# Attention out of PSUM by pairs of banks, part of the second product in whole float32, and a new order

## The chip, the cores and the metric

The kernel runs on one core of a Trainium2 chip. TensorE multiplies matrices and writes only to PSUM, which has eight banks of 512 float32 columns on 128 partitions. VectorE and ScalarE read PSUM and SBUF, GpSimd (POOL) works on SBUF here, and SyncE issues the transfers (DMA). The engines run side by side, each executes its own list in order, and they wait for each other by semaphores. The metric is the device time of one execution in microseconds (us).

## The reference

```python
def _attn_ref(q, k, v, f_logit):          # 4 batches, 8 heads, 768 steps, 48 wide
    f = 1.0 / (1.0 + np.exp(-f_logit))
    for t in range(S):
        state = f[:, :, t, :, None] * state + np.einsum('bhd,bhe->bhde', k[:, :, t], v[:, :, t])
        y[:, :, t] = np.einsum('bhd,bhde->bhe', q[:, :, t], state)
    return y

def _moe_ref(x, w_in, w_out):             # x: 3072 x 384; w_in: 384 x 2048; w_out: 2048 x 384
    h = x @ w_in
    relu6 = np.clip(h + 3.0, 0.0, 6.0)
    return ((h * relu6 / 6.0) @ w_out).astype(np.float32)
```

The heads of the attention's output, side by side, are `x`. `q`, `k`, `v` and `f_logit` come as float32, both weights as float64.

## The kernel before, in words

**Attention.** The 768 steps are cut into six chunks of 128, and a chunk of one batch is a *unit*: 24 units, numbered chunk by chunk with the four batches inside. A unit is prepared by loads (`load` of the gates, `loadq` of q and k, `loadv`), a sigmoid on ScalarE (`gate`), two scans over the gates on VectorE (`back`, `fwd`), their ends (`rend`), products of keys and queries with the scans (`kmul`, `qmul`), and the decay of the old state (`decay`). On TensorE it then has five steps in plain float32, each of small matmuls on a quarter of the array: `tk` (keys transposed), `kv` (the state's additions), `qs` (queries with the state), `att` (keys with queries) and `av` (the masked result with the values, added onto what `qs` left in PSUM). `ktok` copies the transposed keys out on ScalarE. `mask0` and `mask1` multiply each half of `att`'s result with the causal mask on VectorE. `carry0` and `carry1` add the halves of `kv` to the state, two instructions each, on VectorE (on ScalarE for the first four units).

**Out of PSUM.** The expert layer wants its numbers as a pair of the shorter float32 form (`F32R`): a high part, copied on ScalarE, and a low part, subtracted on VectorE. A unit's output `y` lies in two banks and leaves in three pieces: `xh0`, `xh1`, `y3h` copy (256, 128 and 128 columns) and `xl0`, `xl1`, `y3l` subtract. The last piece goes to a tile of its own, `y3`, from which two DMAs (`hole`) fill the 16 unused rows on two places of the other blocks, so that 4 x 96 rows fill three blocks of 128.

**Expert layer.** The four units of a chunk make a *group* of 512 columns, and there are 6 groups x 16 slices of the hidden width = 96 slices, numbered through. Each has a first product `mm1` (nine matmuls: high x high, high x low and low x high over three blocks), `relu` on ScalarE, `g` on VectorE, the high and low parts of the result (`gh` on ScalarE, `gl` on VectorE), and a second product `mm2` (nine matmuls into three banks that add up over a group). At the end `outs`, `outv` and `od` copy and store; the last group's third output block is split into halves (`mm2a`, `mm2b`).

**Weights.** While the first group runs, 16 slices of float64 weights are turned into pairs: `ld` loads 768 KB into a ring of three buffers, `z` and `cy` (ScalarE) and `mid`, `lim`, `dif`, `top` (VectorE) build the float32 number by integer arithmetic in place, `high` copies the high part on ScalarE and `low` subtracts the low part on VectorE or POOL. A load waits until the `low` that last used its buffer is done.

**Order.** Nothing is scheduled while the kernel is built: the string `ORDER` lists every step, and each engine executes its own in that order. `ON_POOL` names the vector steps that go to GpSimd. The digits behind a TensorE step name the PSUM banks that it writes (five banks, `g0` to `g4`; three more hold the second products' sums). `warm.n` puts n bfloat16 matmuls on zeros into TensorE's list. A step whose bank, tile or input is still in use waits for it.

Of the kernel before, what the change touches and what calls it, by code (L numbers as in the profile page):

```python
# [39 lines left out]
kmul.1 qmul.1 kmul.3 qmul.3 kmul.4 qmul.4 kmul.5 gl.0 decay.5 low.3 kmul.6 decay.6 low.9 kmul.7 decay.7 qmul.7  # L40
kmul.8 gl.13 qmul.8 kmul.9 decay.9 gl.17 kmul.10 kmul.11 qmul.11 qmul.10 kmul.12 decay.12 kmul.13 qmul.13
kmul.14 qmul.14 kmul.15 qmul.15 decay.16 qmul.17 gl.46 gl.51 kmul.19 qmul.19 decay.20 kmul.21 qmul.21 kmul.23
qmul.22 decay.23 qmul.23
""".split()
ORDER = """
load.0 loadq.0 load.1 loadv.0 loadq.1 loadv.2 loadv.1 gate.0 loadq.2 back.0 rend.0 kmul.0 gate.1 fwd.0 warm.13
tk.0.0 ktok.0 kv.0.12 qmul.0 load.2 back.1 carry0.0 carry1.0 qs.0.34 att.0.01 rend.1 kmul.1 mask0.0 loadq.3
mask1.0 av.0 fwd.1 tk.1.2 xh1.0 loadv.3 xh0.0 y3h.0 ktok.1 y3l.0 load.3 qmul.1 xl1.0 xl0.0 kv.1.01 hole.0 gate.2
carry0.1 back.2 carry1.1 warm.2 qs.1.24 ld.0 att.1.30 kmul.2 loadq.4 rend.2 tk.2.1 fwd.2 ktok.2 gate.3 qmul.2
load.4 mask0.1 mask1.1 warm.6 kv.2.13 back.3 av.1 carry0.2 ld.1 xh1.1 y3h.1 rend.3 cy.0 y3l.1 kmul.3 xl1.1  # L50
warm.2 qs.2.04 z.0 fwd.3 xh0.1 carry1.2 mid.0 warm.3 att.2.13 load.5 qmul.3 xl0.1 gate.4 mask0.2 hole.1 tk.3.2
mask1.2 ktok.3 lim.0 av.2 dif.0 loadq.6 kv.3.13 xh0.2 top.0 ld.2 xh1.2 y3h.2 carry0.3 loadv.4 carry1.3 xl0.2
loadv.5 cy.1 xl1.2 qs.3.21 y3l.2 att.3.30 back.4 hole.2 high.0 z.1 low.0 loadq.5 gate.5 mid.1 kmul.4 mask0.3
mask1.3 warm.9 av.3 ld.3 lim.1 tk.4.4 dif.1 y3h.3 loadv.6 xh0.3 ktok.4 top.1 xh1.3 xl1.3 high.1 y3l.3 xl0.3
warm.4 kv.4.30 rend.4 cy.2 hole.3 low.1 z.2 fwd.4 mid.2 load.6 decay.4 qmul.4 carry0.4 ld.4 carry1.4 lim.2
warm.15 qs.4.41 dif.2 att.4.20 top.2 loadq.7 mask0.4 high.2 mask1.4 back.5 cy.3 warm.4 av.4 mm1.0.3 loadv.7
xh1.4 xh0.4 low.2 z.3 xl0.4 kmul.5 y3h.4 ld.5 gate.6 xl1.4 y3l.4 hole.4 mm1.2.2 relu.0 mid.3 lim.3 g.0 dif.3
gh.0 top.3 mm1.1.0 relu.2 g.2 gl.0 cy.4 gh.2 rend.5 mm2.0 relu.1 gl.2 z.4 g.1 decay.5 gh.1 mid.4 lim.4 tk.5.4
high.3 gl.1 ktok.5 dif.4 mm2.1 low.3 mm2.2 top.4 ld.6 fwd.5 cy.5 mm1.3.1 high.4 qmul.5 load.7 z.5 low.4 mid.5
ld.7 mm1.4.3 lim.5 relu.3 dif.5 g.3 top.5 gh.3 kv.5.20 relu.4 gl.3 high.5 g.4 mm2.3 cy.6 low.5 gh.4 carry0.5  # L60
ld.8 z.6 gl.4 mm1.5.4 gate.7 mid.6 lim.6 dif.6 top.6 mm2.4 relu.5 back.6 high.6 cy.7 low.6 qs.5.13 z.7 g.5
kmul.6 ld.9 carry1.5 gh.5 mm1.6.4 mid.7 gl.5 lim.7 dif.7 mm2.5 top.7 relu.6 g.6 high.7 rend.6 gh.6 low.7
att.5.02 cy.8 tk.6.4 gl.6 ld.10 z.8 mask0.5 decay.6 mm2.6 mask1.5 ktok.6 mid.8 lim.8 dif.8 top.8 av.5 fwd.6
mm1.7.0 loadv.8 high.8 cy.9 low.8 load.8 z.9 qmul.6 mm1.8.2 ld.11 relu.7 mid.9 lim.9 xh1.5 y3h.5 g.7 xh0.5 dif.9
gh.7 kv.6.40 top.9 relu.8 gate.8 gl.7 high.9 g.8 mm2.7 cy.10 low.9 carry0.6 y3l.5 xl0.5 gh.8 xl1.5 carry1.6 z.10
hole.5 qs.6.21 gl.8 ld.12 mm1.9.3 mid.10 lim.10 dif.10 top.10 mm2.8 relu.9 back.7 high.10 g.9 cy.11 kmul.7
att.6.04 gh.9 low.10 tk.7.3 z.11 loadq.8 loadq.9 gl.9 ktok.7 ld.14 mid.11 mm1.10.3 lim.11 dif.11 top.11 mask0.6
mm2.9 relu.10 mask1.6 high.11 g.10 gh.10 low.11 cy.12 kv.7.04 gl.10 ld.13 mm1.11.3 z.12 rend.7 fwd.7 mid.12
load.9 decay.7 mm2.10 relu.11 lim.12 qmul.7 carry0.7 g.11 gh.11 dif.12 av.6 top.12 xh1.6 loadv.9 xh0.6 gl.11
high.12 back.8 mm2.11 cy.13 low.12 z.13 gate.9 kmul.8 xl1.6 ld.15 xl0.6 mm1.12.3 y3h.6 carry1.7 y3l.6 mid.13  # L70
hole.6 lim.13 dif.13 top.13 qs.7.20 relu.12 att.7.41 g.12 high.13 loadq.10 mask0.7 tk.8.3 cy.14 low.13 gh.12
mask1.7 mm1.13.4 z.14 gl.12 ktok.8 mid.14 lim.14 dif.14 av.7 relu.13 top.14 kv.8.13 y3h.7 loadv.10 xh1.7 xh0.7
mm2.12 g.13 high.14 xl0.7 gh.13 low.14 cy.15 y3l.7 gl.13 mm1.14.4 xl1.7 z.15 hole.7 mid.15 lim.15 dif.15 mm2.13
relu.14 top.15 g.14 high.15 rend.8 mm1.16.2 gh.14 low.15 gl.14 decay.8 fwd.8 mm1.15.0 relu.16 g.16 qmul.8
load.10 carry0.8 gh.16 carry1.8 mm2.14 relu.15 gl.16 g.15 back.9 gh.15 mm1.17.4 gate.10 gl.15 rend.9 kmul.9
mm2.15 relu.17 decay.9 g.17 fwd.9 gh.17 mm1.18.2 outs.0 outv.1 gl.17 outs.2 load.11 od.0 od.1 qmul.9 mm2.16 od.2
relu.18 back.10 g.18 kmul.10 gate.11 mm2.17 gh.18 back.11 gl.18 mm1.19.1 rend.11 decay.11 mm2.18 relu.19 g.19
gh.19 mm1.20.3 gl.19 mm2.19 relu.20 g.20 gh.20 mm1.21.0 gl.20 mm2.20 relu.21 g.21 gh.21 qs.8.42 gl.21 att.8.13
tk.9.0 mask0.8 loadq.11 mask1.8 ktok.9 mm1.22.1 av.8 relu.22 kv.9.30 xh1.8 loadv.11 g.22 xh0.8 mm2.21 y3h.8
# [20 lines left out]
g.43 qmul.17 load.19 tk.15.4 mm1.44.2 ktok.15 gh.43 rend.18 decay.18 gl.43 av.14 kv.15.34 relu.44 gate.19 g.44  # L100
mm2.43 loadv.17 y3h.14 xh0.14 carry0.15 gh.44 xl0.14 xh1.14 gl.44 xl1.14 y3l.14 mm1.45.2 back.19 hole.14
carry1.15 mm2.44 relu.45 g.45 gh.45 tk.16.1 gl.45 qs.15.03 att.15.42 ktok.16 mask0.15 mm1.46.1 mask1.15 av.15
kv.16.42 relu.46 g.46 xh1.15 mm2.45 xh0.15 xl1.15 gh.46 carry0.16 xl0.15 y3h.15 gl.46 y3l.15 carry1.16 hole.15
# [58 lines left out]
def gla_moe(ctx: ExitStack, tc: tile.TileContext, fg, qk, v, w, outT):  # L162
# [5 lines left out]
    )  # L168
    cv = Ring(ctx.enter_context(tc.tile_pool(name="cv", bufs=1)), {"raw": 3, "y": 1})
# [4 lines left out]
    def bank(shape, name):  # L174
# [621 lines left out]
```

## Time and profile before

| | us |
|---|---|
| median of 3 runs | 520.85 |
| lowest and highest run | 518.43, 521.64 |
| span of the profiled execution | 519.0 |
| TensorE (PE) busy in that span | 499.7 |
| VectorE (DVE) busy | 316.3 |
| ScalarE (ACT) busy | 215.5 |
| GpSimd (POOL) busy | 55.5 |

For the profiled execution the page gives its span, from the first to the last instruction, and no time beside it; the span lies between the lowest and the highest run. A line of the page names the line of the kernel, the engine, the operation, output and input, the shapes and the count; then come the busy time, the mean of one instruction in ns, and the idle time just before with what ended it. PE is matmuls and PEld weight loads, which overlap them. The span of a matmul in the records is longer than its share of TensorE's time, because matmuls are pipelined; the distance from start to start is that share.

### The profile page before, as it was taken

The page shows a single profiled execution, that of the slowest core. Times are in us where ns is not written, and L with a number is a line of the kernel's source. Part 1 is how long each engine was busy: PE and PEld are TensorE (multiplying, and loading weights), DVE is VectorE, ACT ScalarE, POOL GpSimd, SP SyncE. Part 2 cuts the span into 40 slices and gives each one's busy share as a digit, 9 for nine tenths or more (in the row PEclk, how much of TensorE's full clock was granted, in tenths as well). Part 3 has the DMA queues.
Part 4 walks back from the last instruction along what each step waited for, and adds up shares of the span by engine and source line. Part 5 has one row for each costly group of instructions (what it writes and reads, how often), then busy time and mean ns, then how long its engine had stood idle before and what let it go on. Part 6 is the DMA issues. An engine that isn't in the chain of part 4 may idle for free.

```text
span 519.0 us, 11607 instructions
## 1 busy us (share of the span) xinstructions
PE 499.7 (96%) x4931; PEld 391.9 (76%) x4931; DVE 316.3 (61%) x599; ACT 215.5 (42%) x390; POOL 55.5 (11%) x61
## 2 busy tenths in 40 slices
PE   7889999989999999999999999999999999999995
PEld 3556777668877777888788778778777778888884
DVE  6799999998936768334783476547364333333331
ACT  3466676666433434333333343334233233433341
POOL 3213111212202112000200002000040000000000
PEclk9799999989999999999999999999999999999998
DMA  8886445741204223300320422111230000200002
GB/s 240 242 259 204 140 134 165 255 125 42 80 1 123 53 65 92 97 0 25 98 70 16 115 77 58 39 52 35 64 105 11 12 1 8 62 1 2 0 1 66
DMA packets 24554, 41.97 MB, mean 81 GB/s; under 512 B 2480, under 2 KB 17072, under 8 KB 24496
## 3 DMA queue, kind: packets, MB, share of 16 engines
q1 hardware_dynamic: 24496, 41.15, 26.9%
q8 instruction: 41, 0.67, 0.6%
q14 instruction: 17, 0.14, 0.1%
HBM read 34.07 MB, written 4.72 MB: 75 GB/s over the span
## 4 chain that ended last, share of the span: by engine, by line
PE 82%; DVE 8%; ACT 4%; issue 3%; DMA 1%; SPq 0%; POOL 0%; DVEq 0%; ACTq 0%; POOLq 0%
PE h L528 36%; PE o L565 33%; PE y L465 3%; PE o_half L577 2%; PE y L451 2%; PE at L378 2%; PE tk L400 2%; PE kv L419 2%; DVE raw L263 1%; DMA raw<-w 1%; PE idle L660 1%; ACT top L243 1%; ACT weight L268 1%; DVE gg L551 1%; DVE top L259 1%
## 5 line engine op out<-in xcount | busy, mean ns | idle before, releaser
L528 PE MATMUL h<-xt,weight 128*128 128x512 f32 x864 | 220.5, 401 | 2.2 <-ACT raw L234 1.2
L565 PE MATMUL o<-gg,weight 128*128 128x512 f32 x816 | 208.7, 399 | 0.3 <-ACT gg L547 0.3
L528 PEld LDWEIGHTS h<-xt,weight 128*128 128x128 f32 x864 | 160.8, 190 | 40.7 <-ACT top L243 1.3
L565 PEld LDWEIGHTS o<-gg,weight 128*128 128x128 f32 x816 | 151.4, 188 | 36.8 <-DVE gg L551 0.4
L542 DVE SCALAR_TENSOR_TENSOR tg<-tg,h 128x512 f32<-128x512 f32 x96 | 65.9, 686 | 123.7 <-ACT tg L538 123.3
L538 ACT ACTIVATE tg<-h,half 128x512 f32<-128x512 f32 x96 | 66.1, 688 | 178.7 <-PE h L528 176.9
L551 DVE TENSOR_TENSOR gg<-tg,gg 128x512 fp32r<-128x512 f32 x94 | 65.9, 701 | 40.9 <-ACT gg L547 36.9
L547 ACT ACTIVATE gg<-tg 128x512 fp32r<-128x512 f32 x96 | 60.6, 632 | 58.2 <-DVE tg L542 57.4
L326 POOL TENSOR_TENSOR qkf<-qkf,suffix 112x512 f32<-112x512 f32 x17 | 23.2, 1363 | 249.1 <-DVE tg L542 96.1
L313 DVE TENSOR_TENSOR_SCAN suffix<-gates,unit 112x516 f32<-112x516 f32 x24 | 30.3, 1261 | 3.0 <-ACT gates L307 2.8
L333 DVE TENSOR_TENSOR_SCAN suffix<-gates,rend 112x516 f32<-112x516 f32 x24 | 30.1, 1253 | 0.8 <-POOL qkf L326 0.5
L339 POOL TENSOR_TENSOR qkf<-qkf,suffix 112x512 f32<-112x512 f32 x15 | 18.0, 1202 | 42.9 <-DVE suffix L333 39.2
L388 DVE TENSOR_TENSOR a<-at,causal 128x256 f32<-128x256 f32 x48 | 18.1, 416 | 7.3 <-PE at L378 7.1
L465 PEld LDWEIGHTS y<-a,v 64*48 64x48 f32 (+1 forms) x768 | 13.4, 124 | 10.8 <-issue 6.2
L407 ACT ACTIVATE ktok<-tk 128x448 f32<-128x448 f32 (+1 forms) x24 | 12.3, 512 | 19.5 <-PE tk L400 19.4
L465 PE MATMUL y<-a,v 64*48 64x64 f32 (+1 forms) x768 | 17.5, 225 | 2.1 <-DVE a L388 2.0
L263 DVE SCALAR_TENSOR_TENSOR raw<-top,raw 128x768 int16<-128x768 int16 x16 | 18.2, 1138 | 0.5
L378 PE MATMUL at<-qkf 48*64 48x64 f32 x768 | 17.1, 227 | 1.4 <-ACT state L438 1.4
L660 PE MATMUL idle<-blank 128*128 128x512 bf16 x58 | 17.2, 445 | 1.1 <-DVE blank L198 1.1
L268 ACT ACTIVATE weight<-raw 128x768 fp32r<-128x768 f32 x16 | 13.5, 845 | 10.8 <-DVE raw L263 10.8
L496 ACT ACTIVATE xt<-y 112x128 fp32r<-112x128 f32 (+1 forms) x48 | 14.0, 327 | 9.1 <-PE y L465 9.1
L419 PE MATMUL kv<-v,ktok 64*48 64x48 f32 (+1 forms) x768 | 16.2, 216 | 1.6 <-ACT ktok L407 1.4
(61 smaller groups left out, 307.9 us busy)
## 6 DMA issues: line engine op xcount, KB each, us to landing
raw<-w SPq DMA_DIRECT2D x16, 768.0 KB, 5.2
qkf<-qk SPq DMA_DIRECT2D x24, 448.0 KB, 4.4
gates<-fg SPq DMA_DIRECT2D x24, 226.2 KB, 2.9
v<-v SPq DMA_DIRECT2D x24, 200.0 KB, 3.5
outT<-os SPq DMA_DIRECT2D x17, 256.0 KB, 3.1
xt<-y SPq DMA_DIRECT2D x48, 48.0 KB, 2.2
outT<-os SPq DMA_DIRECT2D x2, 128.0 KB, 3.4
```

The lines of the kernel that those rows point to most:

```text
L263: nc.vector.scalar_tensor_tensor(upper, conv[f]["y"], 8.0, upper, op0=ALU.mult, op1=ALU.add)
L313: nc.vector.tensor_tensor_scan(flat(sf)[:, ::-1], gt[:, 1:][:, ::-1], flat(unit)[:, ::-1], 0.0, op0=ALU.mult, op1=ALU.add,)
L333: nc.vector.tensor_tensor_scan(flat(sf), gt[:, :NP * (C + 1)], flat(rend), 0.0, op0=ALU.mult, op1=ALU.add,)
L378: nc.tensor.matmul(d["ps"][e][HC * odd:HC * (odd + 1), 2 * n + c], t[rs, 1, n, c, odd], t[rs, 0, n, c, odd], start=True, stop=True,)
L419: nc.tensor.matmul(d["kv"][odd][r:r + m, c, n], d["ktok"][rs, 2 * n + part, r:r + m], heads_of(vt[rs], part, n, e)[:, :D], start=(odd, e) ...
L465: nc.tensor.matmul(d["y"][odd][to:to + m, n, cs], heads_of(vt[rs], c, n, e)[:, :m], d["a"][rs, 2 * n + c, e], start=False, stop=True, skip ...
L528: nc.tensor.matmul(h, win[:, f, a, k * 128:(k + 1) * 128], g["xt"][:, k, :g["n"] // C, b], start=i == 0, stop=i == 3 * KT - 1,)
L538: nc.scalar.activation(d["t"], d["h"], AF.Relu, bias=half, scale=1.0 / 6.0)
L542: nc.vector.scalar_tensor_tensor(d["t"], d["t"], 1.0, d["h"], op0=ALU.min, op1=ALU.mult)
L547: nc.scalar.activation(d["gg"][:, 0], d["t"], AF.Copy)
L551: engine("gl", f if g["name"] == "0" else NU).tensor_tensor(d["gg"][:, 1], d["t"], d["gg"][:, 0].bitcast(F32), op=ALU.subtract)
L565: nc.tensor.matmul(g["o"][m], wout[:, f, a, m * 128:(m + 1) * 128], g[f]["gg"][:, b], start=f == 0 and i == 0, stop=f == NF - 1 and i == 2 ...
```

## The change

The five working banks become one tile `work`, and steps take one bank or two neighbouring ones of it. The two banks of `att`, of `kv` and of `y` are such pairs, so that one instruction reads both: `mask` takes the place of `mask0` and `mask1`, `xh` of three copies, `xl` of three subtractions, and `carry0` and `carry1` have one instruction instead of two. `y` uses columns 0 to 255 of its pair and `kv` columns 256 to 447 of its pair, and the order puts both into banks 0 and 1 for most units. The piece that fills the unused rows goes to a fourth block of the group's input. All blocks lie in one tile of seven, of which even groups use the first four and odd ones the last four from the end, so the middle one belongs to both. `decayed` has two buffers instead of one for each batch. `av` begins with an instruction that does nothing and waits until `qs` is done.

In the first eight slices of the first group, `mm2x` takes the place of `gh`, `gl` and `mm2`: three matmuls in whole float32, of the gated result itself and whole weights. For them the DMA `wd` puts the second half of a slice's float32 weights where its low part will be, `lowi` makes the low part of the first half, and `lowo` later makes that of the second half in place. The raw ring has two buffers instead of three, and the float32 weights get two of their own.

The order and `ON_POOL` are new. Fillers (`warm`) go from 58 to 46. Steps that issued transfers stay one for one, but for eight `wd` that are added, and stand at other places. Of the vector steps `kmul` 13 (before 17), `qmul` 13 (15), `decay` 13 (8), two `gl` (2), two `low` (2), two `lowi` and one `lowo` are on POOL.

```diff
-        {"qkf": 3, "v": 3, "ktok": 2, "y3": 2, "tg": 4, "gg": 3, "a": 1, "xt": 2},
+        {"qkf": 3, "v": 3, "ktok": 2, "tg": 4, "gg": 3, "a": 1},
-    cv = Ring(..., {"raw": 3, "y": 1})
+    cv = Ring(..., {"raw": 2, "w": 2, "y": 1})
+    work = ps_g.tile([128, 5, 512], F32, name="work")
+    def bank():
+        return work[:, banks.pop(0) if banks else 0]
+    def pair():
+        n = banks.pop(0) if banks else 0
+        return work[:, n:n + 2]
...
+    def conv_low(op, f, cols, whole):
+        engine(op, f).tensor_tensor(
+            weight[:, f, 1, cols], whole, weight[:, f, 0, cols].bitcast(F32), op=ALU.subtract
+        )
+    def conv_keep(f):
+        nc.sync.dma_start(out=weight[:, f, 1, OUTS].bitcast(F32), in_=conv[f]["w"][:, OUTS])
+        "low": lambda f: conv_low("low", f, slice(0, WN), conv[f]["w"]),
+        "lowi": lambda f: conv_low("lowi", f, INS, conv[f]["w"][:, INS]),
+        "lowo": lambda f: conv_low("lowo", f, OUTS, weight[:, f, 1, OUTS].bitcast(F32)),
...
-        def mask(e):
+        def mask():
+            nc.vector.tensor_tensor(
+                d["a"].rearrange("r p e t -> r e p t"), d["at"],
+                causal.unsqueeze(1).unsqueeze(1).broadcast_to([128, 2, NP, HC]), op=ALU.mult,
+            )
...
+            d["kv"] = pair()[:, :, 256:256 + 4 * D].rearrange("r o (c n d) -> r o c n d", c=2, n=2)
+            d["y"] = pair()[:, :, :2 * C].rearrange("r o (n t) -> r o n t", t=C)
...
         def av():
             vt = values[i]
+            hold = nc.tensor.nop()
+            after(hold.ins, d["qs"], mybir.DependencyClass.Sync)
...
+        def parts(low):
+            return rows_of(g)[:PR, :, j, low].rearrange("r (n o) t -> r o n t", o=2)
+        def xh():
+            nc.scalar.activation(parts(0), d["y"][:PR], AF.Copy)
+        def xl():
+            nc.vector.tensor_tensor(parts(1), d["y"][:PR], parts(0).bitcast(F32), op=ALU.subtract)
...
+            g["xt"] = xts[:, KT:][:, ::-1] if g["odd"] else xts[:, :KT + 1]
...
+    def mm2_whole(g, f):
+        for m in range(KT):
+            nc.tensor.matmul(
+                g["o"][m], wout[:, f, 1, m * 128:(m + 1) * 128].bitcast(F32), g[f]["t"],
+                start=f == 0, stop=f == NF - 1, skip_group_check=True,
+            )
```

Of the order, the start, the stretch around units 8 to 10, and that around unit 18; in the old order the first product stood behind `warm.4 av.4`:

```diff
+load.0 loadq.0 loadv.0 loadq.1 load.1 loadv.1 loadv.2 gate.0 loadq.2 back.0 ld.0 ld.1 rend.0 kmul.0 warm.15 tk.0.4
...
+xh.3 xl.3 high.1 back.4 hole.3 gate.5 wd.1 cy.2 ld.3 lowi.1 loadv.6 mid.2 lim.2 warm.10 mm1.0.4 dif.2 top.2 ld.4
+back.5 high.2 wd.2 mm1.1.0 relu.0 lowi.2 g.0 kmul.5 cy.3 rend.4 mm1.2.4 relu.1 kmul.4 z.3 g.1 decay.4 mid.3 mm2x.0
...
+att.9.2 decay.10 loadq.11 av.8 gl.21 kv.9.0 loadv.11 mask.9 mm2.20 xh.8 carry0.9 xl.8 carry1.9 hole.8 qs.9.0 kmul.11
+att.10.2 loadq.12 decay.11 av.9 fwd.11 kv.10.0 tk.11.4 xh.9 mm2.21 rend.12 load.13 ktok.11 xl.9 qmul.11 hole.9
...
+att.18.2 loadq.20 av.17 kv.18.0 decay.19 mask.18 loadv.20 mm2.57 xh.17 carry0.18 xl.17 carry1.18 hole.17 tk.19.4 gh.58
+kmul.20 qs.18.0 ktok.19 gl.58 att.19.2 loadq.21 fwd.20 av.18 kv.19.0 mm2.58 xh.18 carry0.19 qmul.20 load.22 mask.19
```

More of the change, by code (lines that the diff above doesn't have):

```diff
@@ L44 @@
+kmul.18 qmul.18 decay.19 qmul.20 decay.21 kmul.22 qmul.22 decay.22 kmul.23 qmul.23 lowo.2 lowi.6 lowi.7 low.9 low.13
+gl.14 gl.15
 """.split()
 ORDER = """
[L46 to L79, printed above, removed]
@@ L100 @@
[L100 to L103, printed above, removed]
-mm1.47.1 mm2.46 relu.47 g.47 gh.47 mm1.48.0 gl.47 mm2.47 relu.48 g.48 gh.48 qs.16.32 att.16.41 outs.6 gl.48
@@ L140 @@
-mm2m1.93 mm2m1.94 mm2m0.95 mm2m1.95 outs.15 mm2a.93 od.15 outv.16 mm2a.94 mm2a.95 od.16 mm2b.93 outh.15 mm2b.94
-odh.15 mm2b.95 outh.16 odh.16
+load.0 loadq.0 loadv.0 loadq.1 load.1 loadv.1 loadv.2 gate.0 loadq.2 back.0 ld.0 ld.1 rend.0 kmul.0 warm.15 tk.0.4
+fwd.0 ktok.0 qmul.0 load.2 warm.1 kv.0.0 gate.1 att.0.2 carry0.0 back.1 carry1.0 qs.0.0 loadq.3 mask.0 kmul.1 rend.1
+warm.2 av.0 fwd.1 xh.0 tk.1.4 ktok.1 xl.0 warm.1 kv.1.2 qmul.1 hole.0 load.3 att.1.0 z.0 loadv.3 mask.1 cy.0 carry0.1
+mid.0 warm.3 qs.1.0 carry1.1 lim.0 av.1 loadq.4 dif.0 z.1 top.0 gate.2 back.2 high.0 wd.0 loadv.4 xh.1 ld.2 rend.2
@@ new lines @@
+kmul.2 cy.1 xl.1 gate.3 hole.1 fwd.2 warm.10 tk.2.4 ktok.2 qmul.2 load.4 warm.1 kv.2.0 back.3 att.2.2 carry0.2
+carry1.2 mid.1 qs.2.0 mask.2 kmul.3 loadq.5 rend.3 warm.1 av.2 fwd.3 tk.3.4 xh.2 loadv.5 ktok.3 xl.2 qmul.3 warm.1
+kv.3.2 hole.2 carry0.3 load.5 lim.1 att.3.0 carry1.3 lowi.0 gate.4 qs.3.2 mask.3 z.2 loadq.6 dif.1 warm.1 av.3 top.1
+xh.3 xl.3 high.1 back.4 hole.3 gate.5 wd.1 cy.2 ld.3 lowi.1 loadv.6 mid.2 lim.2 warm.10 mm1.0.4 dif.2 top.2 ld.4
+back.5 high.2 wd.2 mm1.1.0 relu.0 lowi.2 g.0 kmul.5 cy.3 rend.4 mm1.2.4 relu.1 kmul.4 z.3 g.1 decay.4 mid.3 mm2x.0
@@ new lines @@
+lim.3 relu.2 dif.3 g.2 ld.5 z.4 top.3 fwd.4 mm2x.1 high.3 wd.3 cy.4 lowi.3 load.6 mid.4 lim.4 dif.4 mm1.3.4 top.4 ld.6
+z.5 lowo.1 wd.4 lowo.0 mm2x.2 relu.3 qmul.4 cy.5 g.3 high.4 mid.5 lim.5 gate.6 dif.5 mm2x.3 lowo.2 rend.5 ld.7 top.5
+fwd.5 cy.6 wd.5 att.4.2 tk.4.4 high.5 lowi.4 tk.5.1 load.7 mm1.4.0 decay.5 mask.4 z.6 lowi.5 ktok.4 mid.6 ktok.5 lim.6
+z.7 dif.6 mm1.5.4 top.6 relu.4 g.4 high.6 wd.6 ld.8 back.6 mm2x.4 relu.5 cy.7 g.5 lowi.6 gate.7 rend.6 mid.7 lim.7
+mm1.6.4 dif.7 top.7 qmul.5 wd.7 kv.4.0 relu.6 ld.9 back.7 mm2x.5 high.7 cy.8 g.6 lowi.7 carry0.4 z.8 carry1.4 kmul.6
@@ new lines @@
+mm1.7.4 mid.8 lim.8 dif.8 top.8 ld.10 mm2x.6 relu.7 fwd.6 high.8 z.9 g.7 qmul.6 load.8 cy.9 rend.7 qs.4.0 low.8
+att.5.2 loadq.7 av.4 mid.9 kv.5.0 decay.6 mask.5 loadv.7 z.10 mm1.8.4 lim.9 xh.4 dif.9 gate.8 top.9 ld.11 tk.6.2
+carry0.5 kmul.7 cy.10 mm2x.7 carry1.5 xl.4 ktok.6 fwd.7 high.9 hole.4 relu.8 mid.10 load.9 low.9 g.8 kv.6.0 qs.5.2
+gh.8 carry0.6 carry1.6 av.5 loadq.8 qs.6.0 loadv.8 lim.10 z.11 gl.8 mm1.9.4 xh.5 dif.10 gate.9 decay.7 xl.5 ld.12
+top.10 hole.5 tk.7.2 relu.9 mm2.8 qmul.7 high.10 g.9 cy.11 low.10 gh.9 mm1.10.4 mid.11 ktok.7 gl.9 lim.11 z.12 dif.11
@@ L374, in att @@
             t = chunks[i]
-            d["ps"] = [bank([128, NP, HC], f"at{i}_{e}") for e in range(2)]
+            d["at"] = pair()[:, :, :NP * HC].rearrange("r e (p t) -> r e p t", t=HC)
             for n, c, odd, e in tiles(range(2)):
@@ L573, in half_mm2 @@
         if f == 0:
-            g["oh", part] = bank([128, 512], f"o_half{part}")[:, :n]
+            g["oh", part] = bank()[:, :n]
         for i in range(3):
@@ L656, in gla_moe @@
         i = int(i)
-        banks[:] = "".join(tail)
+        banks[:] = map(int, tail)
         if op == "warm":
```

271 lines of the change are left out of this document (120 added, 151 removed).

## The prediction

> **What bounds the kernel now.** I began with the page's head, its busy row and its slices, and then asked for the busy time of the engines in five stretches. I cut the stretches at the first product of the expert layer (43.63 us), at the last visible gap of TensorE (117.72), at the end of the first group's sixteenth second product (134.69) and at the last matmul (512.75). In a stretch row the first figure is the length; then come PE, PEld, DVE, ACT and POOL busy, the clock and the DMA share.
>
> ```profile
> span 519.0 us, 11607 instructions
> PE 499.7 (96%) x4931; PEld 391.9 (76%) x4931; DVE 316.3 (61%) x599; ACT 215.5 (42%) x390; POOL 55.5 (11%) x61
> ...
> 0.00:43.63 43.63, 35.78 (x719) 21.82 (x719) 35.42 (x69) 20.96 (x51) 9.47 (x23) 0.92 0.86 252
> 43.63:117.72 74.09, 69.13 (x671) 53.04 (x667) 71.19 (x126) 51.19 (x81) 14.99 (x11) 0.98 0.51 161
> 117.72:134.69 16.97, 16.97 (x75) 13.67 (x73) 15.08 (x29) 9.64 (x16) 4.82 (x4) 1.00 0.12 32
> 134.69:512.75 378.06, 377.85 (x3476) 303.39 (x3474) 194.62 (x378) 133.33 (x244) 26.26 (x23) 1.00 0.17 47
> ```
>
> There are two kernels here. From 117.72 us on TensorE is never idle (377.85 of 378.06), so there only TensorE work counts, and vector instructions saved are worth nothing. Before 43.63 no product runs at all, and from there to 117.72 VectorE is the fuller engine: 71.19 of 74.09 us (96%) against 93% for TensorE.
>
> Next I priced TensorE work from the chain that ended last and from TensorE's instructions in order of time (start, length, what).
>
> ```profile
> 183.44 2.11 PE o L565 x9
> 186.64 2.29 PE h L528 x9
> ...
> 185.48 0.46 PE L451 MATMUL y<-qkf,decayed 48*64 48x64 f32 x16
> 185.99 0.65 PE L378 MATMUL at<-qkf 48*64 48x64 f32 x32
> 186.57 2.36 PE L528 MATMUL h<-xt,weight 128*128 128x512 f32 x9
> 188.86 0.66 PE L465 MATMUL y<-a,v 64*48 64x64 f32 x32
> 189.35 0.63 PE L419 MATMUL kv<-v,ktok 64*64 64x48 f32 x32
> 189.91 2.37 PE L565 MATMUL o<-gg,weight 128*128 128x512 f32 x9
> ...
> 193.30 0.60 PE L400 MATMUL tk<-ident,qkf 112*128 112x112 f32 x4
> 193.68 2.34 PE L565 MATMUL o<-gg,weight 128*128 128x512 f32 x9
> ```
>
> A product (nine matmuls) takes 2.11 us when it follows another, and 2.29 just after attention matmuls: a change of kind costs about 0.2. From start to start a unit of attention takes 0.51 (`qs`), 0.58 (`att`), 0.49 (`av`), 0.56 (`kv`) and 0.38 (`tk`), 2.52 us in all; 2.05 in the last four units, which do half of `kv` and `tk`.
>
> The start of the run is read from these rows, TensorE first and then VectorE and SyncE:
>
> ```profile
> 35.84 3.41 PE L660 MATMUL idle<-blank 128*128 128x512 bf16 x15
> 42.71 0.99 PE L465 MATMUL y<-a,v 64*48 64x64 f32 x32 [0.46 <-DVE a L388]
> 43.63 1.19 PE L528 MATMUL h<-xt,weight 128*128 128x512 f32 x4
> ...
> 35.38 0.42 DVE L502 TENSOR_TENSOR xt<-y,xt 112x256 fp32r<-112x256 f32 x1
> 35.86 1.22 SPq L508 DMA_DIRECT2D xt<-y  x2
> ...
> xt<-y SPq DMA_DIRECT2D x48, 48.0 KB, 2.2
> ```
>
> The group's inputs were complete at about 39.3 us (vector work ends at 35.8, two issues of 1.22 together, 2.2 to land). The order puts unit 4's attention ahead of the first product, so that begins at 43.63.
>
> The whole span as a TensorE account: 192 products x 2.11 = 405.1; attention 20 x 2.52 + 4 x 2.05 = 58.6; 53 places in the order where attention is next followed by a product x 0.2 = 10.6; before the first product, less the attention done there (four units and all of unit 4 but `av`: 12.1), 31.5 of filler matmuls and waiting; the tail after the last matmul 6.2. That is 512.0. The 7.0 left to 519.0 is waiting and stretched matmuls, nearly all between 43.63 and 134.69: the order does 83.0 us of work there in 91.1.
>
> **The change part by part.**
>
> ```profile
> L551 DVE TENSOR_TENSOR gg<-tg,gg 128x512 fp32r<-128x512 f32 x94 | 65.9, 701 | 40.9 <-ACT gg L547 36.9 <-PE o_half L577 2.1 <-PE o L565 1.4
> L547 ACT ACTIVATE gg<-tg 128x512 fp32r<-128x512 f32 x96 | 60.6, 632 | 58.2 <-DVE tg L542 57.4 <-PE o L565 0.4
> L388 DVE TENSOR_TENSOR a<-at,causal 128x256 f32<-128x256 f32 x48 | 18.1, 416 | 7.3 <-PE at L378 7.1
> L502 DVE TENSOR_TENSOR xt<-y,xt 112x128 fp32r<-112x128 f32 (+1 forms) x48 | 16.2, 353 | 1.2 <-ACT y L482 0.8 <-ACT xt L496 0.3
> L485 DVE TENSOR_TENSOR y<-y,y 112x128 fp32r<-112x128 f32 x24 | 6.8, 285 | 0.6 <-ACT y L482 0.6
> L313 DVE TENSOR_TENSOR_SCAN suffix<-gates,unit 112x516 f32<-112x516 f32 x24 | 30.3, 1261 | 3.0 <-ACT gates L307 2.8
> L271 DVE TENSOR_TENSOR weight<-raw,weight 128x768 fp32r<-128x768 f32 x14 | 14.9, 1067 | 1.2 <-ACT weight L268 0.9
> L432 DVE TENSOR_TENSOR middle<-kv,decayed 112x96 f32<-112x96 f32 x40 | 8.3, 251 | 3.4 <-PE kv L419 3.3
> ```
>
> *Pairs of banks.* No 512-column instruction here spans two banks. The nearest is the 512-column subtraction at 701 ns; below it, half lengths without the second fixed part; above it, two halves as now. I take 0.70. Per unit VectorE then saves 2 x 0.416 - 0.70 = 0.13 on the mask and 2 x 0.353 + 0.285 - 0.70 = 0.29 on the low parts. The four 251-ns additions become two of twice the width, about 0.36 each between the 251 at 96 columns and the 416 at 256: 0.28 saved. This counts only while VectorE leads, about eight units; later TensorE covers it.
>
> *First product earlier.* Up to the fourth unit's low part the new order has on VectorE four fewer 0.42s (1.7), one scan less (1.26), and in place of one whole low part of weights (1.07) a half-width one, estimated at 0.6 (0.45): 3.4 us (one key product fewer and one query product more on VectorE cancel). Its vector work so ends at 32.4 instead of 35.8, and with issue and landing the first product starts at 36.0, since unit 4 is moved behind it. Before the product remain 36.0 - 4 x 2.52 = 25.9 us against 31.5: **5.6 saved**. Fillers drop from 58 to 46; they stand in waits, so I count none apart.
>
> *Whole float32.* Eight second products become three float32 matmuls each; the low and high halves of the activations go (8 x 0.632 on ScalarE, 8 x 0.701 on the vector side), and the product waits on the gate alone. The trace has no float32 matmul of 512 columns; the nearest rows:
>
> ```profile
> L528 PE MATMUL h<-xt,weight 128*128 128x512 f32 x864 | 220.5, 401 | 2.2 <-ACT raw L234 1.2 <-ACT ktok L407 0.6 <-DVE a L388 0.2
> L577 PE MATMUL o_half<-gg,weight 128*128 128x256 f32 x96 | 13.6, 280 | 0.0
> L378 PE MATMUL at<-qkf 48*64 48x64 f32 x768 | 17.1, 227 | 1.4 <-ACT state L438 1.4
> ```
>
> A float32 attention matmul appears as two records (768 for 24 units of 16), each longer than one pass would be: 227 ns at 64 columns, where the one-pass rows (401 at 512, 280 at 256) extrapolate to 159 + 64 x 0.47 = 189. If a record is two passes, a product is twelve: at the fillers' 214 ns (3.41 us for 15, less overlap) 2.57, at the product's own 234, 2.81. The upper end is the latencies' slope, (227 - 159)/64 = 1.06 ns a column, 3.26; the lower end is the 0.58/32 us of a small record taken eight times, six times over: 0.87, which counts tiles that run side by side as if serial. I take 2.69, between the two middle ones: 8 x 0.58 = **4.6 lost**, from 10 gained to 9 lost at the ends.
>
> *Weights.* Each whole second half goes by DMA (196 KB, eight) and is reduced later on VectorE (seven of about 0.6; one on POOL); the raw ring falls from three buffers to two, the halves being converted into two new ones. SyncE waits in order, so a late join holds each queued load behind it. I charge nothing but keep a rival.
>
> *The order.* Places where attention gives way to a product fall from 53 to 37: **3.2 saved**. Between the first product and the sixteenth second one TensorE has 27 x 2.11 + 8 x 2.69 + 4 x 2.52 + 9 x 0.2 = 90.4 us of work; VectorE has 83 (mean durations summed over the order, scaled by 0.93 because that sum over the whole order gives 340 against the page's 316.3). Before it was 83.0 against 83.5. TensorE is now the fuller one, and its second products wait less; I take 3.0 of the old waiting away.
>
> *Shared banks.*
>
> ```profile
> 21.30 0.45 PE L451 MATMUL y<-qkf,middle 48*64 48x64 f32 x12 [0.39 <-DVE xt L502]
> ```
>
> Here `qs` waited 0.39 us for a low part, the last reader of a bank it writes. Now `kv` and `y` of nearly every unit lie in banks 0 and 1, in columns of their own, so if the bank is what is guarded the next `qs` follows the high part, the low part and both carries, about 0.63 + 0.70 + 2 x 0.36 + signals = 2.5 us. In three places (units 9, 12, 18) little more than one product of 2.11 covers that: **1.5 lost** at 0.5 each. The nop ahead of `av` waits for `qs`; in 15 units other TensorE work lies between; in nine `qs` is next to it, four of them before the first product, and the other five I count at nothing, at most a drain of 0.3 each.
>
> The Trainium skill, "PSUM — Partial Sum Buffer", section "PSUM bank collisions raise a hardware error", says that two engines on one bank must be ordered even where their columns differ. The row agrees that a reader is waited for and cannot show differing columns; guarded by columns the 1.5 would be nothing, guarded by that rule it stands, and the first rival below is its other direction.
>
> Sum: 519.0 - 5.6 + 4.6 - 3.2 - 3.0 + 1.5 = 513.3, that is 5.7 less. The span stands 1.85 below the median of 520.85; what lies around it I leave alone, so **515** for the median. About 1% (5.2 us) is what a measurement can tell from no change.
>
> **The rivals.**
>
> *Slower, by the bank chain.* In twelve places of the new order TensorE has `av` of one unit directly before `kv` of the next, in the same two banks. If `kv` must wait for both readers of `y`, each place costs 0.63 + 0.70 and signals, 1.7 us: 20 us, so about 534. It decides as soon as a bank, not its columns, is what is guarded, and the readers come first. For it is the row of `qs` above, which waited on a reader. Against it: the order lists `kv` ahead of the readers, so with a guarded bank these wait for `kv`, which is what I have charged. Chance 0.07.
>
> *Slower, by the two raw buffers.*
>
> ```profile
> raw<-w SPq DMA_DIRECT2D x16, 768.0 KB, 5.2
> DMA to landing us min/median/max: 4.3/5.2/9.0
> L263 DVE SCALAR_TENSOR_TENSOR raw<-top,raw x16: 1011/1046/2586, 26.9 to 122.6; 128x768 int16<-128x768 int16 x16
> 54.12 2.59 DVE L263 SCALAR_TENSOR_TENSOR raw<-top,raw 128x768 int16<-128x768 int16 x1
> 53.70 2.09 POOL L271 TENSOR_TENSOR weight<-raw,weight 128x768 fp32r<-128x768 f32 x1 [2.63 <-ACT weight L268]
> ```
>
> Between a raw load's release and its first use lie 5 to 8 us of VectorE work. At 5.2 to land that holds; at 8, about eight loads come 1.7 late, 14 us: 527 to 529. The DMA share of 0.86 up to 43.63, and loads planned still earlier, speak for it. POOL adds to it: the join of 2.59 us, against a median of 1.05, began 0.4 us into a POOL subtraction and ended after it, and five subtractions of weights are on POOL in this stage (two before). Chance 0.14.
>
> *No gain.* Float32 at 3.26 (4.6 more), or a paired instruction costing as much as its halves (first product 1.7 later, VectorE full again): 518 to 522. This is also the case that joining doesn't do what it says. Chance 0.20.
>
> *Better.* Float32 at 2.57 and 3 us less waiting: 507 to 511. Chance 0.14.
>
> **How the numbers follow.** My forecast, 511 to 519, has 0.45, of which 0.27 lies below 515.6. Faster by over 1%: 0.27 + 0.14 = 0.41; within: 0.18 + 0.20 = 0.38; slower: 0.21. The range from 507 to 527 leaves out the bank chain, the worst of the loads and a little below.
>
> **What would show it.** First product at 36 us (right within 2); a whole-float32 product of three matmuls at 2.6 to 2.8; the mask and low part near 0.70; no visible TensorE gap above 0.6 after 135 us. Wrong if ScalarE waits on raw loads at L234 or L243, if `kv` or `qs` waits on the low part by more than 0.5 in many units, or if the joined instructions exceed 0.8.

## The result, and the profile after

The changed kernel takes a median of **661.28 us** (657.92 to 666.78) beside 520.25 us for the one before on the same chip: 1.272 times as long, 95% interval 1.265 to 1.279. The forecast was 515, the range 507 to 527. The size of the miss, 146 us, says that some mechanism was left out, not that a term was a little off. Times are medians over all executions of a kernel; one of the six of the last kernel below (five tiles) took 962.08 us, which nothing here explains, and its ratio is formed without that one.

The page of the changed kernel: its span, busy times, and two rows of its 40 slices (each digit is tenths busy), then the shares of the chain that ended last.

```profile
span 664.7 us, 11371 instructions
PE 538.8 (81%) x4895; PEld 395.6 (60%) x4895; DVE 305.3 (46%) x489; ACT 206.4 (31%) x326; POOL 55.5 (8%) x61
...
PE   6779897878896777879798976887887888699985
DVE  5758785786676542435313231474232222323222
...
PE 64%; DVE 14%; ACT 12%; issue 5%; DMA 3%; SPq 1%; POOL 0%; ACTq 0%; DVEq 0%; POOLq 0%
```

VectorE and ScalarE have less to do than before (305.3 and 206.4 us against 316.3 and 215.5), so what was to be removed was removed. Yet TensorE, which before was hardly ever idle from 118 us to the last matmul, now stands at six to nine tenths nearly from end to end, while VectorE is mostly at one to four tenths in the last two thirds: there **nobody is full, everybody waits**. The chain that ended last passes through VectorE and ScalarE for 26% of the span.

The busy times of the engines in three stretches (length, then PE, PEld, DVE, ACT, POOL, clock, DMA share): up to the first product, to 155.28 (the start of the fifteenth second product), and to 658.00, just ahead of the last six matmuls.

```profile
0.00:43.90 43.90, 31.18 (x575) 18.05 (x575) 27.98 (x46) 17.72 (x32) 6.91 (x19) 0.81 0.72 208
43.90:155.28 111.38, 92.35 (x802) 61.84 (x803) 79.10 (x132) 54.80 (x77) 17.84 (x14) 0.95 0.42 141
155.28:658.00 502.72, 414.26 (x3515) 314.93 (x3513) 197.97 (x312) 133.49 (x216) 30.71 (x28) 0.95 0.13 36
```

After 155 us TensorE is idle for 502.72 - 414.26 = 88 us, where the row of before from 134.69 to 512.75 left 0.2. Of whom each engine waits for, the waits answer (total us, times, longest):

```profile
ACT tg L526 <- PE work L516: 175.3, 61, 9.9
DVE tg L530 <- ACT tg L526: 156.4, 62, 9.9
PE work L516 <- DVE tg L530: 40.1, 26, 2.5
```

L516 is the first product `mm1`, L526 `relu`, L530 `g`. That `mm1` waits for `g` is new: the list of before has no such row. The instructions in order of time show which `g` it waits for (start, length, engine, line, operation, in brackets the idle time before it and who ended that). The order here, other steps left out, is `mm1.15.4 mm1.16.3 relu.15 g.15 mm1.17.2 relu.16 g.16 mm1.18.4`, the last digit being the bank.

```profile
143.19 4.52 PE L516 MATMUL work<-xts,weight 128*128 128x512 f32 x18
147.75 0.69 ACT L526 ACTIVATE tg<-work,half 128x512 f32<-128x512 f32 x1 [4.04 <-PE work L516]
148.47 0.69 DVE L530 SCALAR_TENSOR_TENSOR tg<-tg,work 128x512 f32<-128x512 f32 x1 [0.72 <-ACT tg L526]
149.21 2.37 PE L516 MATMUL work<-xts,weight 128*128 128x512 f32 x9 [1.50 <-DVE tg L530]
151.61 0.69 ACT L526 ACTIVATE tg<-work,half 128x512 f32<-128x512 f32 x1 [1.79 <-PE work L516]
152.33 0.69 DVE L530 SCALAR_TENSOR_TENSOR tg<-tg,work 128x512 f32<-128x512 f32 x1 [2.17 <-ACT tg L526]
153.07 2.36 PE L516 MATMUL work<-xts,weight 128*128 128x512 f32 x9 [1.50 <-DVE tg L530]
```

The first row is two products, `mm1.15` into bank 4 and `mm1.16` into bank 3. `relu.15` reads bank 4, complete after half of that row, and starts only when both are done. Then `mm1.17`, which writes bank 2, starts only when `g.15` has read bank 4; and so on with `relu.16` (bank 3), `g.16` and `mm1.18` (bank 4). In none of these waits between a matmul and a read do the two touch one bank. What they share is the tile `work`: a read waits for every matmul on it that the order lists ahead, a matmul for every such read. So the chain product, `relu`, `g`, product runs in single file, 149.21 to 153.07 = **3.86 us** a slice, of which TensorE works 2.37, wherever no second product stands between.

### The profile page after: what moved, and what is told of

The parts are those of the page before. It is cut to its first block, busy times and chain, and to the rows that moved or that the text cites. A ratio compares the mean times of both kernels' runs of the same rounds, so it can differ in the third digit from the quotient of the medians.

```text
span 664.7 us, 11371 instructions
## 1 busy us (share of the span) xinstructions
PE 538.8 (81%) x4895; PEld 395.6 (60%) x4895; DVE 305.3 (46%) x489; ACT 206.4 (31%) x326; POOL 55.5 (8%) x61
## 4 chain that ended last, share of the span: by engine, by line
PE 64%; DVE 14%; ACT 12%; issue 5%; DMA 3%; SPq 1%; POOL 0%; ACTq 0%; DVEq 0%; POOLq 0%
PE work L516 34%; PE o L553 19%; DVE tg L530 7%; ACT tg L526 7%; DMA qkf<-qk 3%; PE work L578 2%; PE work L453 2%; PE work L470 2%; PE work L403 2%; PE work L422 2%; PE work L384 2%; DVE xts L492 1%; ACT xts L489 1%; DVE a L391 1%; ACT ktok L410 1%
## 5 line engine op out<-in xcount | busy, mean ns | idle before, releaser
L516 PE MATMUL work<-xts,weight 128*128 128x512 f32 x864 | 234.9, 420 | 68.6 <-DVE tg L530 40.1
L516 PEld LDWEIGHTS work<-xts,weight 128*128 128x128 f32 x864 | 165.0, 198 | 125.7 <-DVE tg L530 52.1
L553 PE MATMUL o<-gg,weight 128*128 128x512 f32 x744 | 189.8, 405 | 0.7 <-ACT gg L535 0.3
L530 DVE SCALAR_TENSOR_TENSOR tg<-tg,work 128x512 f32<-128x512 f32 x96 | 65.7, 685 | 195.9 <-ACT tg L526 156.4
L526 ACT ACTIVATE tg<-work,half 128x512 f32<-128x512 f32 x96 | 65.9, 686 | 214.5 <-PE work L516 175.3
L391 DVE TENSOR_TENSOR a<-work,causal 128x512 f32<-128x512 f32 x24 | 16.5, 688 | 29.6 <-PE work L422 13.1
L492 DVE TENSOR_TENSOR xts<-work,xts 112x512 fp32r<-112x512 f32 x24 | 16.5, 686 | 21.9 <-ACT xts L489 13.5
L422 PE MATMUL work<-v,ktok 64*48 64x48 f32 (+1 forms) x768 | 17.2, 225 | 11.0 <-DVE tg L530 4.0
L566 PE MATMUL o<-tg,weight 128*128 128x512 f32 x48 | 23.7, 636 | 1.9 <-DVE tg L530 1.9
L470 PE MATMUL work<-a,v 64*48 64x64 f32 (+1 forms) x768 | 17.4, 234 | 4.9 <-ACT tg L526 2.2
```

Of the source, the lines that this page charges most:

```text
L422: nc.tensor.matmul(d["kv"][r:r + m, odd, c, n], d["ktok"][rs, 2 * n + part, r:r + m], heads_of(vt[rs], part, n, e)[:, :D], start=(odd, e) ...
L470: nc.tensor.matmul(d["y"][to:to + m, odd, n, cs], heads_of(vt[rs], c, n, e)[:, :m], d["a"][rs, 2 * n + c, e], start=False, stop=True, skip ...
L516: nc.tensor.matmul(h, win[:, f, a, k * 128:(k + 1) * 128], g["xt"][:, k, :g["n"] // C, b], start=i == 0, stop=i == 3 * KT - 1,)
L526: nc.scalar.activation(d["t"], d["h"], AF.Relu, bias=half, scale=1.0 / 6.0)
L530: nc.vector.scalar_tensor_tensor(d["t"], d["t"], 1.0, d["h"], op0=ALU.min, op1=ALU.mult)
L553: nc.tensor.matmul(g["o"][m], wout[:, f, a, m * 128:(m + 1) * 128], g[f]["gg"][:, b], start=f == 0 and i == 0, stop=f == NF - 1 and i == 2 ...
```

## The experiments

The theory (A): the tile is what is guarded, not its banks or columns. Rivals: the new order itself, the shared columns of a pair, the whole float32 product, or the wide instructions. All kernels of this section compute the whole reference.

**Three tiles.** The joined tile is cut into two pairs and a single bank; nothing else is changed.

```diff
-    work = ps_g.tile([128, 5, 512], F32, name="work")
+    pair0 = ps_g.tile([128, 2, 512], F32, name="pair0")
+    pair2 = ps_g.tile([128, 2, 512], F32, name="pair2")
+    bank4 = ps_g.tile([128, 512], F32, name="bank4")
```

> The changed kernel with its five working banks as three PSUM tiles (banks 0 and 1, banks 2 and 3, bank 4) instead of one; order, banks and instructions are the same. Theory A (every read of the one tile waits for every matmul on that tile listed ahead of it, and every matmul for every read listed ahead, whatever the bank): the waits between different tiles go, the 1.50-us gaps between first products go with them, and the time falls from 661 to my old forecast, 516 (505 to 530). Rival B (the new order itself, by true reuse of banks, buffers and engines): nothing changes, 640 or more. Rival C (the start: two raw buffers, whole float32): TensorE's idle 32 us before 155 us stays and only part of the rest goes, 540 to 600.

Measured: 524.59 us, ratio to before 1.0093 (1.0061 to 1.0125). That is within the range of theory A and outside those of rivals B and C. Three lines, and the two helpers that hand out banks, take back 137 of the 141 us.

**The old kernel with one tile.** Before's order, banks and instructions; only its five bank tiles are views of one.

```diff
+    work = ps_g.tile([128, 5, 512], F32, name="work")
     def bank(shape, name):
-        return ps_g.tile(shape, F32, tag=f"g{banks.pop(0) if banks else 0}", name=name)
+        one = work[:, int(banks.pop(0)) if banks else 0]
+        ...
```

> The kernel before with only its five working banks made one PSUM tile; order, instructions and banks as before. Theory A: slower although nothing else changes. In the old order a second product of 2.11 us mostly stands between a read's listing and the next first product, so plain stretches lose little, but each of about 50 attention blocks waits 0.5 to 1.5 us for reads of other banks: 545 to 600. Rivals B and C: 520, because neither the order nor the weights' buffers are touched.

Measured: 638.45 us, ratio 1.2297 (1.2244 to 1.2350). That is above the range that I expected. Its page, then, in order of time, the same three links of the chain, and three of its waits:

```profile
span 636.1 us, 11605 instructions
PE 533.1 (84%) x4931; PEld 401.3 (63%) x4931; DVE 316.5 (50%) x599; ACT 216.1 (34%) x390; POOL 56.1 (9%) x61
```

```profile
161.39 0.69 ACT L545 ACTIVATE tg<-work,half 128x512 f32<-128x512 f32 x1
162.11 0.69 DVE L549 SCALAR_TENSOR_TENSOR tg<-tg,work 128x512 f32<-128x512 f32 x1
162.85 2.37 PE L535 MATMUL work<-xt,weight 128*128 128x512 f32 x9 [1.49 <-DVE tg L549]
```

```profile
PE work L535 <- DVE tg L549: 8.5, 7, 1.5
PE work L535 <- DVE state L447: 8.5, 5, 1.9
PE work L535 <- DVE a L395: 6.6, 9, 1.1
```

The gap of 1.49 before a product that follows a `g` is the one of the changed kernel. Here it is rare: seven waits, 8.5 us. As expected, plain stretches lose little; from 259.01 to 284.31 us, where second products stand between, one product starts every 2.11. The loss lies around the attention blocks, and there I had sized it too low: first products wait for sums of states (`carry1`, L447) and for masks (L395), and attention steps for reads of other steps in the same way. TensorE is idle for 103.0 us of the span (636.1 - 533.1) against 19.3 before, and its matmuls are busy for 33.4 more. The same instructions on the same banks cost 118.6 us more (638.45 against 519.89): the wait is made by how the tile is declared, not by the banks. With the run of three tiles this shows A from both sides.

**Three tiles without the whole float32 product.** `mm2x`, `wd`, `lowi` and `lowo` become `gh`, `gl`, `mm2` and `low` again.

```diff
-mm2x.0   lowi.0   wd.0
+gh.0 gl.0 mm2.0   low.0
...
```

> Three tiles as in e1, and the whole-float32 second products undone: the eight slices have gh, gl and mm2 again, one low instead of lowi, lowo and wd, at the same places. Theory A: whole float32 is no cause of the loss; TensorE has 8 x 0.5 = 4 us less work, VectorE 5 us more in a stage where it is nearly full, so within 4 us of e1. Rival C (whole float32 or the weights' copies cost the start): 10 us or more faster than e1.

Measured: 530.52 us, ratio 1.0226 (1.0199 to 1.0253): 6 us *slower*, more than I had expected of it. The stretch from the first product to that of slice 16, first with whole float32 (run of three tiles), then without:

```profile
40.56:121.20 80.64, 79.16 (x775) 55.51 (x776) 74.76 (x125) 52.40 (x74) 17.58 (x13) 1.00 0.60 195
```

```profile
38.65:126.40 87.75, 77.43 (x798) 59.29 (x799) 79.00 (x130) 57.45 (x82) 18.90 (x12) 1.00 0.50 164
```

Without it TensorE has 1.7 us less to do and takes 7.1 longer: VectorE has 79.00 instead of 74.76, and TensorE waits 10.3 us instead of 1.5. Rival C, which expected a gain of 10 us or more, falls.

**Three tiles, halves again.** `mask`, `xh` and `xl` as two instructions, one for each bank.

```diff
-            nc.scalar.activation(parts(0), d["y"][:PR], AF.Copy)
+            for o in range(2):
+                nc.scalar.activation(parts(0)[:, o], d["y"][:PR, o], AF.Copy)
```

> Three tiles as in e1, with the mask, the high part and the low part each made of two instructions, one for each bank, instead of one. Joining saves 2 x 0.416 - 0.69 = 0.14 us on the mask and as much on the low part, which counts in about eight units: 2 us slower than e1 (0 to 4). If the joined form is what slows PSUM down, e4 is faster than e1.

Measured: 523.38 us, ratio 1.0084 (1.0058 to 1.0110). Against three tiles with joined instructions there is no difference that can be told (522.43 to 526.70 there, 520.51 to 527.61 here): of the 2 us that I expected from joining these three, nothing is seen, and the joined form is not what is slow.

**Three tiles, the end on other banks.** What does the run with three tiles still lose to the forecast? Here is its last group, from the first product of slice 80 to the last matmul, as a stretch and then two instructions out of it in order of time:

```profile
440.54:518.96 78.42, 75.63 (x355) 60.93 (x355) 26.53 (x43) 23.84 (x37) 0.00 (x0) 0.98 0.05 14
```

```profile
452.69 1.65 PE L581 MATMUL pair<-gg,weight 128*128 128x256 f32 x6 [1.20 <-ACT tg L529]
453.80 0.69 DVE L533 SCALAR_TENSOR_TENSOR tg<-tg,pair 128x512 f32<-128x512 f32 x1 [2.86 <-PE pair L581]
```

L581 is `mm2a` and `mm2b`, the halves' sums, in banks 3 and 1; `relu.81` (L529) and `g.81` (L533) read bank 2. `mm2a.80` waits 1.20 for `relu.81`, and `g.81` then 2.86 for `mm2a.80`, on another bank of the same pair. So a pair still makes false waits within itself. The edit moves the last group's first products to banks 2 and 4, the halves' sums to 0 and 1.

```diff
-mm1.81.2 ... mm2a.80.3 g.81 mm2b.80.1 ... mm1.82.0 ... mm1.84.2
+mm1.81.2 ... mm2a.80.0 g.81 mm2b.80.1 ... mm1.82.4 ... mm1.84.4
...
-mm2b.93 outh.15 mm2b.94 odh.15 mm2b.95 outh.16 odh.16
+mm2b.93 mm2b.94 mm2b.95 outh.15 outh.16 odh.15 odh.16
```

> The joined instructions and the three tiles of the run with three tiles stay; only the last group's use of banks changes: its first products alternate banks 2 and 4, its two halves' sums lie in banks 0 and 1, and the second half's last products go before the first store of that half. Theory (the whole tile is guarded): the last group, 78.5 us with three tiles against 69.8 before, loses 8.7 us because a halves' sum shares a tile with a first product's bank; without that sharing it takes about 70, and the run 524.6 - 8.7 + 0.5 (three second products moved ahead of two stores) = 516.5 us, between 514 and 519. Rival (only the order of the end, or two banks for the first products, is slow): the last group stays above 77 us and the run at 523 to 526.

Measured: 520.91 us, ratio 1.0018 (0.9997 to 1.0039). The last two stretches of it, before and after slice 80:

```profile
129.28:438.08 308.80, 302.66 (x3149) 241.95 (x3146) 166.98 (x264) 106.82 (x176) 31.50 (x28) 1.00 0.20 55
438.08:511.61 73.53, 72.43 (x355) 59.90 (x355) 26.18 (x42) 23.84 (x37) 0.00 (x0) 1.00 0.05 15
```

The last group falls from 78.4 to 73.5 us, neither to the 70 of the theory nor above 77: both expectations missed. I had compared with 69.8 before, but the new order has one second product more behind `mm1.80` (2.1), so only 78.4 - 69.8 - 2.1 = 6.5 us could be waits, and 4.9 of that went. Not all of the 4.9 is the edit's: the last group of the two other runs with three tiles takes 76.95 us (without whole float32) and 76.97 (halves) at a clock of 1.00, while the 78.42 was at 0.98. Against those it is 3.4.

**Five tiles.** Every bank a tile of its own, with the new order and its banks; all that was joined becomes two instructions.

```diff
+    five = [ps_g.tile([128, 512], F32, name=f"bank{n}") for n in range(5)]
...
-        return work[:, n:n + 2]
+        return five[n:n + 2]
```

> Every bank is a tile of its own, with the new order and the banks it plans; mask, copies out, low parts and sums of states run as two instructions, one for each bank, since no tile holds two banks. Theory (the whole tile is guarded, and nothing else is wrong with the new order): no wait is left between different banks, the last group takes about 70 us, the part before it stays as in the run with three tiles and halves (first second-layer group of the end near 438 us), and the time is 514 to 518 us, what was forecast for the change. Rival (the new order itself loses time): 523 to 526 us, as with three tiles.

Measured: **514.61 us**, ratio 0.9898 (0.9867 to 0.9929), the fastest of all. Its page; then three stretches, cut at the first product, the end of the sixteenth second product and the last matmul, and from the last of them the last group alone; then three of its waits:

```profile
span 512.6 us, 11492 instructions
PE 494.8 (97%) x4895; PEld 383.8 (75%) x4895; DVE 309.0 (60%) x573; ACT 208.4 (41%) x358; POOL 56.3 (11%) x61
```

```profile
0.00:37.84 37.84, 30.48 (x574) 17.94 (x575) 28.48 (x54) 18.70 (x44) 6.91 (x19) 0.86 0.84 241
37.84:129.32 91.48, 89.95 (x821) 63.99 (x822) 85.16 (x157) 57.47 (x86) 19.04 (x15) 1.00 0.51 171
129.32:507.03 377.71, 374.37 (x3502) 301.89 (x3500) 195.40 (x364) 131.87 (x228) 30.32 (x28) 1.00 0.17 48
433.50:507.03 73.53, 72.40 (x355) 59.94 (x355) 26.71 (x43) 24.06 (x38) 0.00 (x0) 1.00 0.06 15
```

```profile
ACT w L227 <- DMA raw<-w: 5.0, 4, 2.1
...
PE bank L524 <- DMA xts<-xts: 2.7, 1, 2.7
...
PE o L561 <- ACT gg L543: 1.1, 1, 1.1
```

TensorE's idle time after 129 us is back to 3.3 us. So the order, the banks it plans (`kv` and `y` of most units still lie in one pair of banks, in columns of their own), the whole float32 product and the weights' new path are all sound together; what made the change slow was one declaration, which the joined instructions asked for. Against three tiles with halves, 8.8 us are gone (523.38 to 514.61), though the two ran beside different runs of before (519.89 and 520.11); apart from the tiles only the sums of states differ, which are halves here too.

The time fell into the expected range by two errors that cancel. The last group takes 73.5 us, not 70, but it starts at 433.5 us, not near 438. It is as long as in the run with the end on other banks (73.53), so in the last group that run seems to have had no false wait left; beyond 69.8 + 2.1 there are 1.1 of the wait on `gg` in the list above and 0.5 more. What five tiles take away beyond that run lies ahead of slice 80: from the sixteenth second product to there they need 304.2 us, with TensorE idle for 2.2 (377.71 - 374.37 less the 1.1), against 308.8 and 6.1 in that run.

## Why the prediction was wrong

**The step that failed is "Shared banks".** It asked whether a bank or its columns is guarded, priced the worse at 0.5 us in each of three places, 1.5 in all, and counted nothing elsewhere. The thing guarded was larger than both: all five banks. The row it leaned on (`qs` waiting 0.39 us for a low part) is explained as well by a tile, since before a bank *was* a tile; I read "the last reader of a bank" where the row could only say "of a tile". The sentence on the joined tile was in my own description of the change, and I did not follow what it does to `mm1`, `relu` and `g`, which touch no pair. It could have been sized roughly: `relu` and `g` take 0.69 each, with signals 1.50 in which no first product may run. That 96 slices of this are 144 us, near the 141 that the change cost, is a coincidence: the waits list 26 gaps of `mm1` behind a `g`, 40.1 us. The span grew by 145.7 us (519.0 to 664.7): 106.6 of it is idle time of TensorE (125.9 against 19.3), in which waits for masks, low parts, copies of keys and sums of states, all reads of the tile, stand beside those for `g`; 39.1 is longer busy time of its matmuls, at a mean granted clock of 0.937 against 0.987.

**The rival "by the bank chain" had the right kind of mechanism and far too small a place**: twelve places of 1.7 us, 534, at a chance of 0.07. Its point of decision (a whole bank is guarded) is not what decided. Its argument against, that the order lists `kv` ahead of the readers, was right for one pair and didn't ask what those readers then wait for.

**The Trainium skill's rule** in "PSUM — Partial Sum Buffer", section "PSUM bank collisions raise a hardware error", orders two engines on one bank. The runs do not contradict it, and the loss does not rest on it: in the old kernel with one tile, banks and instructions are those of before, and the 118.6 us come from waits between different banks.

The other steps can be read where the single file is absent, in the runs with separate tiles:

- *Pairs of banks.* The sizes were right. These are groups of the changed kernel (busy, mean ns, idle before):

```profile
L391 DVE TENSOR_TENSOR a<-work,causal 128x512 f32<-128x512 f32 x24 | 16.5, 688 | 29.6 <-PE work L422 13.1 <-PE work L516 6.6 <-PE work L453 3.9
L492 DVE TENSOR_TENSOR xts<-work,xts 112x512 fp32r<-112x512 f32 x24 | 16.5, 686 | 21.9 <-ACT xts L489 13.5 <-PE work L516 4.0 <-ACT ktok L410 3.5
L437 DVE TENSOR_TENSOR middle<-work,decayed 112x192 f32<-112x192 f32 x20 | 7.0, 356 | 24.8 <-ACT xts L489 12.4 <-PE work L516 5.0 <-PE work L470 3.2
```

  0.688 and 0.686 for 0.70, 0.356 for 0.36. What they save did not reach the time, as the run with halves shows.
- *First product earlier.* Forecast 36.0 within 2; 37.84 with five tiles, but 43.90 in the changed kernel, whose attention ran in the same single file; `kv.3` (banks 2 and 3) there waits for `xl.2` (banks 0 and 1), in order of time:

```profile
33.41 0.91 PE L422 MATMUL work<-v,ktok 64*64 64x48 f32 x48 [1.63 <-DVE xts L492]
```

  With five tiles the last wait before it is for the DMA that fills the rows, 2.7 us. This start scatters: two profiled runs that are the same up to there (three tiles, and three tiles with the end on other banks) begin the first product at 40.56 and 38.48.
- *Whole float32.* Forecast 2.69 us a product. In the run with five tiles, in order of time:

```profile
68.94 2.84 PE L574 MATMUL o<-tg,weight 128*128 128x512 f32 x6
71.22 2.65 PE L524 MATMUL bank<-xts,weight 128*128 128x512 f32 x9
73.71 2.74 PE L574 MATMUL o<-tg,weight 128*128 128x512 f32 x6
```

  It starts 2.28 before the next product, which itself takes 2.49 to the next start instead of 2.11: 2.66 in all. The size was right and the sign of the step was not: "4.6 lost" on TensorE stands against 7.1 gained in the stretch where VectorE is nearly full, which `gl` and half a low part leave (74.76 us of work instead of 79.00). I had put that gain into a general 3.0 of waiting. In busy time TensorE's stretches with and without whole float32 differ by 1.7 us only, where 8 x 0.55 would be 4.4; why is open.
- *Waiting and order.* From the first product to the sixteenth second one I priced 90.4 us of work; five tiles take 91.48, so nearly all of the old waiting went, not 3.0 of it. Behind it the run takes 377.71 against 378.06 before. My steps promised 2.3 less: 13 of the changes of kind (2.6) and one product (2.11), against one `tk` and `kv` (0.94) and the shared banks (1.5). The work did shrink: TensorE is busy for 374.37 instead of 377.85, 3.5 less, where 3.8 is promised when the shared banks are left out. But it is idle for 3.3 us instead of 0.2, 1.1 of it in the wait on `gg` at the start of the last group, 0.9 for `g` and 0.8 for a `kmul` on POOL, and I had counted no such waits. None of its waits there is for a low part or a sum of a state, so the 1.5 charged for shared banks is not seen at all.
- *The two raw buffers.* With five tiles ScalarE does wait for raw loads, 5.0 us in four waits of the whole run (L227), as this rival says; but from the first product to the sixteenth second one TensorE is idle for only 1.5 us of 91.48, so they cannot cost the 14 us charged. That rival falls.

With the tile's waits taken out, the sum of 513.3 for the span stands against 512.6. Part of that is luck: by my terms the sixteenth second product ends at 36.0 + 90.4 + 5.1 of waiting left = 131.5, in the run at 129.3, and the rest is 1.9 longer than promised. And five tiles are not the kernel that I forecast, which joins its instructions.

## What to carry to other kernels

Before banks, columns or engines are counted, ask what unit the waits are made from: here a tile of five banks put first products, `relu`, `g` and the attention steps into single file wherever the order lists them side by side, and cutting it took back 137 of 141 us. A tile that spans banks should span only what one instruction must read together, and no bank of it should serve a step with another rhythm; where joining saves 0.15 us on an engine that is not full, separate tiles are worth more. A wait row in a trace names a tile, so before reading it as "the bank" or "the columns", look for a case in which the two differ.

## What the hardware showed unexpectedly

A whole float32 product (three matmuls, six records) holds up the product behind it: in the rows above that takes 2.49 us from start to start where 2.11 is usual. And the granted clock was lower where TensorE waited often: 0.95 in both later stretches of the changed kernel against 1.00 in those of the run with five tiles, and matmuls of `mm1` took 420 ns on average against 399. The old kernel with one tile shows the same: it has the instructions of the old kernel and differs in its waits, and its four executions had a clock of 0.936 to 0.950, thirteen of the old kernel beside it 0.983 to 0.997. So the clock falls with the waits; what about them lowers it is open. The groups of the changed kernel and of the run with five tiles:

```profile
L516 PE MATMUL work<-xts,weight 128*128 128x512 f32 x864 | 234.9, 420 | 68.6 <-DVE tg L530 40.1 <-DVE a L391 8.0 <-DVE xts L492 7.8
```

```profile
L524 PE MATMUL bank<-xts,weight 128*128 128x512 f32 x864 | 213.6, 399 | 4.0 <-DMA xts<-xts 2.7
```
